# A sparse attention and feed-forward kernel: the first 22 loads wait for the one three ahead

## The chip, the cores and the metric

The kernel runs on one core of a Trainium2 chip. The metric is the device time of one execution in microseconds. The five engines of the core are named as in the profile: PE (TensorE; PEld are its weight loads), DVE (VectorE), ACT (ScalarE), POOL (GpSimd) and SP (SyncE). SP only issues transfers here; 16 DMA engines carry them out.

## The reference

Attention over q, k, v of shape (8 batches, 8 heads, 576 positions, 64), then a two-matrix feed-forward block over all 4608 tokens of width 512.

```python
scores = q @ k.T / sqrt(64)
# heads 0-3: 0 <= i - j < 32         (local)
# heads 4-7: i >= j and i % 32 == j % 32   (strided)
attn = softmax(where(mask, scores, -1e9))
x = (attn @ v) as 4608 x 512
h = x @ w_in                       # 512 x 2048
g = where(h >= 1, h, where(h <= -1, 0, (h + 1)**2 / 4))
out = g @ w_out                    # 2048 x 512
```

## The kernel before

All of it runs in one pass over the batches on one core. The queries and keys of a batch come in four tiles (`load_qk`: two for the local heads, two for the strided ones, 576 and 604 KB), the values in four parts for batch 0 (`load_v`: 768, 384, 384 and 320 KB). The weights come as 16 tiles of 128 rows of the hidden layer, each in two halves of 512 KB: half 0 of tile f belongs to w_in, half 1 to w_out (`load_w(f, i)`). They arrive as 64-bit words and are turned into two rounded parts by a chain of five steps on ACT, DVE and POOL: `conv_a` (L457, ACT) and `conv_l` (L461, ACT), `conv_b` (L465, DVE), `conv_c` (L469, POOL), then `conv_d` (L478) and `conv_e` (L482, DVE). Only then can PE use the tile.

Attention of a batch goes score (L592, PE) - mask, maximum, exponential, sum, norm (DVE, ACT, POOL) - transpose (L719, PE) - copy out (L729) - values (L779, PE) - copies into the feed-forward's input, high part (L841, ACT) and low part (L850, DVE). PE then does the first matrix (`up`, L887) and the second (`down`, L947) for the first 512 tokens while further weights are still being converted, and after that the other tokens, in part from combined weight blocks that were stored to DRAM (L1040, L1135). In the first microseconds PE also multiplies zeros (L577, L607).

The order of all instructions is written out by hand: the body runs under a manual schedule, and the long string AGENDA lists the steps with the time at which each is placed between the matrix multiplications. Each engine works through its own queue in that order. All loads are issued by SP, in one queue, in the order in which the program calls them. The first 22 loads are issued ahead of everything else, in this order: the four qk tiles of batch 0; half 0 of weight 0 (it is held until the second qk tile has landed, by a one-element copy on ACT, L435); two parts of v; half 0 of weight 1; two parts of v; half 0 of weight 2; half 1 of weights 0, 1, 2; both halves of weight 3; two qk tiles of batch 1; both halves of weights 4 and 5. The calls are these:

```python
for p in range(4):
    load_qk(0, p)
load_w(0, 0, loaded[0, 1, "qk"][0:1, 0, 0:1])
load_v(0, 0)
load_v(0, 1)
load_w(1, 0)
...
```

In the agenda the conversions by ACT come as A0.0, A1.0, A2.0, A3.0, A0.1, A3.1, A4.0, A1.1 (tile and half); these are its first L457 instructions, in this order.

Of the kernel before, what the change touches and what calls it, by code (L numbers as in the profile page):

```python
# [19 lines left out]
ST = 32  # L20
WR = 7
GATE, ROUNDED = 0.31, 1.62

AGENDA = """
-66.69 0Zs0:17 0o0 0s0 0o1 0i0 0X0 0s1 0i1 0S0 0o3 0g1 0x1 0s2 0Zv0:3 0Zf0:3 0m2 0e0 0a1 A0.0 0s3 0i3 0e1 0x2 0q0
# [263 lines left out]
def tile_sparse_attention_then_ffn(  # L289
# [14 lines left out]
    nc = tc.nc  # L304
# [81 lines left out]
    for i in range(IL):  # L386
        part = slice(i * QL, (i + 1) * QL)
        for n0, n1, off in ((0, SLOTS, ST),) if i else ((0, 1, 0), (1, SLOTS, ST)):
            t = m_loc[part, n0:n1]
# [4 lines left out]
    for i in range(IS):  # L394
        t = m_str[i * QS:(i + 1) * QS]
# [20 lines left out]
    wt, raws, pieces = {}, {}, {}  # L416
    PLACES = (6, 7, 8, 9, 10, 11, 12, 13, 14, 15, 12, 13, 14, 15)
    SUMS_AT = (("X1a", "X1b", "w0", "w1", "w0", "w1", "w0", "w1"), ("X0b", "X0a", "X0b", "X0a", "w11", "w12", "w13", "w14"))
    w_v = w.bitcast(U32).rearrange("f p (i e t) -> f p i e t", i=2, t=2)
# [4 lines left out]
    def place(u, shape, dtype, name):  # L424

        return slot(f"w{u // 2 + NP * (u % 2)}", shape, dtype, name)

    def weight(f, i, h=slice(None)):
        return wt[i, f // 2][:, h, f % 2] if i else wt[i, f // 2][:, f % 2, h]

    def load_w(f, i, after=None):
        if i == 0:
            raws[f] = place(PLACES[f], [P, 2, DM, 2], U32, f"raw_{f}")
        if after is not None:
            nc.scalar.copy(raws[f][0:1, i, 0:1, 0].bitcast(F32), after)  # L435
        nc.sync.dma_start(raws[f][:, i], w_v[f][:, i])
        pieces[f, i] = [(raws[f][:, i], slice(0, DM))]

    def load_piece(f, i, k=0, pool=qk_p, tag="qk", of=1):
# [79 lines left out]
    def load_qk(b, p):  # L519
        src = qk_l[b, p] if p < 2 else qk_s[b, p - 2]  # L520
        if b == 0 and p >= 2:
            t = place(NF + 1 - p, [P, 2, src.shape[2]], F32, f"qk_{b}_{p}")
        else:
            t = qk_p.tile([P, 2, src.shape[2]], F32, tag="qk", name=f"qk_{b}_{p}")
        nc.sync.dma_start(t, src)
        loaded[b, p, "qk"] = t

    def load_v(b, u, k=None):

        local, b0, nb = UNITS[u]  # L530
        if k is not None:
            b0, nb = b0 + k * VB, min(VB, nb - k * VB)
        src = (v_l if local else v_s)[b][:, b0:b0 + nb]
        if b == 0 and u in (0, 3):
            t = place(5 if u else 4, list(src.shape), F32, f"v_{b}_{u}")
        else:
            t = v_p.tile([P, VB, 2, D], F32, tag="v", name=f"v_{b}_{u}_{k}")[:, :nb]
        nc.sync.dma_start(t, src)
        for n in range(nb):
            loaded[b, local, b0 + n] = t[:, n]  # L540

    def fetch_qk(b, p0):
        for p in (p0, p0 + 1):
            if b < B and (b, p, "qk") not in loaded:
                load_qk(b, p)

    def fetch_v(b, *parts):
        for u, k in parts:
            if 0 < b < B and (b, UNITS[u][0], UNITS[u][1] + k * VB) not in loaded:
                load_v(b, u, k)  # L550
# [612 lines left out]
    with tc.manual_schedule():  # L1163
# [6 lines that stand above are left out]
        load_v(0, 2)  # L1170
        load_v(0, 3)
        load_w(2, 0)
        for f in range(3):
            load_w(f, 1)
        for i in range(2):
            load_w(3, i)
        for p in range(2):
            load_qk(1, p)
# [57 lines left out]
        for f in range(NF):  # L1236
            t = 4 * (f - NF)
# [6 lines left out]
        t, last = 0, None  # L1244
# [82 lines left out]
```

## Time and profile before

| | us |
|---|---|
| median of 3 runs | 802.49 |
| lowest, highest run | 801.35, 804.53 |
| span of the profiled execution | 801.3 |
| PE busy | 791.8 (99%) |
| DVE busy | 621.0 (77%) |
| ACT busy | 504.9 (63%) |
| POOL busy | 259.3 (32%) |

The span runs from the first to the last instruction of the one execution that was profiled; its own time outside the span is not listed apart, and the lowest of the runs, 801.35, is next to it. The rows below come from that execution. In a row of an engine the first number is the start in us from the span's start, the second how long the row lasts; in square brackets stands how long the engine was idle before it, and what released it. SPq is SP's issuing of a transfer, not the transfer; the time of a transfer is the time from issue to landing.

### The profile page before, as it was taken

Reading aid. Unit: us, or ns where it says so; the run is one execution under the profiler, and the core shown is the slowest. Engines: PE = TensorE matmul, PEld = TensorE weight load, DVE = VectorE, ACT = ScalarE, POOL = GpSimd, SP = SyncE. Lnnn points to the kernel's source line nnn. Section 1 sums busy time; section 2 is a strip of 40 time slices with the busy share of each in tenths; the row PEclk is TensorE's granted clock in tenths of the full one; section 3 lists DMA queues with packets and bytes.
Section 4 is the critical chain, followed back from the end, with each engine's and each line's share of the span. In section 5 each row is a group of like instructions: output and inputs, shape, how many; then the busy total and the mean of one; then the engine's idle time right before and its main releaser. Section 6 shows DMA issues by size and latency. Waiting matters only on the chain.

```text
span 801.3 us, 17840 instructions
## 1 busy us (share of the span) xinstructions
PE 791.8 (99%) x6921; PEld 647.5 (81%) x6921; DVE 621.0 (77%) x881; ACT 504.9 (63%) x857; POOL 259.3 (32%) x203
## 2 busy tenths in 40 slices
PE   8999999999999999999999999999999999999998
PEld 6778887778887888888888888888888888888886
DVE  5899879998999999978689786675786854566673
ACT  5899854566764555677665456777544667775442
POOL 5456344897584320022141102132424001224000
PEclk9999999999999999999999999999999999999999
DMA  9948888899898999888889778777777676666665
GB/s 347 406 192 292 302 290 303 277 301 309 288 315 302 298 309 361 267 291 273 261 241 309 230 225 268 249 233 214 221 245 244 212 239 193 194 193 188 216 209 164
DMA packets 107699, 209.78 MB, mean 262 GB/s; under 512 B 17760, under 2 KB 33376, under 8 KB 105568
## 3 DMA queue, kind: packets, MB, share of 16 engines
q1 hardware_dynamic: 100560, 179.15, 70.2%
q10 hardware_dynamic: 7056, 29.49, 9.5%
q8 instruction: 55, 0.90, 0.4%
q14 instruction: 28, 0.23, 0.1%
HBM read 161.94 MB, written 46.66 MB: 260 GB/s over the span
## 4 chain that ended last, share of the span: by engine, by line
PE 96%; DMA 1%; DVE 1%; ACT 1%; issue 0%; SPq 0%; DVEq 0%
PE yo L1135 22%; PE y L1040 16%; PE h L887 16%; PE zo L1135 11%; PE z L1040 8%; PE o L947 6%; PE xo L1135 6%; PE x L1040 4%; PE xp L779 4%; PE sc L592 3%; DMA raw<-in_w 1%; DMA qk<-in_qk_l 1%; PE tp L719 1%; DVE xq_b L850 0%; ACT pT L729 0%
## 5 line engine op out<-in xcount | busy, mean ns | idle before, releaser
L1135 PE MATMUL yo<-hl,wr 128*128 128x512 f32 x768 | 177.6, 390 | 0.0
L1135 PEld LDWEIGHTS yo<-hl,wr 128*128 128x128 f32 x768 | 143.6, 188 | 30.8 <-DVE hl L997 0.9
L1040 PE MATMUL y<-x,wr 128*128 128x512 f32 x576 | 139.9, 389 | 0.0
L1040 PEld LDWEIGHTS y<-x,wr 128*128 128x128 f32 x576 | 108.0, 188 | 22.5
L887 PE MATMUL h<-xq_a,w 128*128 128x512 f32 x384 | 123.2, 394 | 1.1 <-DVE g L897 1.0
L1096 POOL TENSOR_TENSOR ga<-gb,ga 128x1024 f32<-128x1024 f32 x17 | 44.1, 2600 | 235.9 <-DVE ga L897 175.5
L997 DVE TENSOR_TENSOR hl<-ga,hl 128x1024 fp32r<-128x1024 f32 x48 | 63.7, 1341 | 36.9 <-ACT hl L996 36.7
L1135 PE MATMUL zo<-hl,wr 128*128 128x512 f32 x384 | 89.3, 391 | 0.0
L887 PEld LDWEIGHTS h<-xq_a,w 128*128 128x128 f32 x384 | 72.0, 188 | 17.3 <-DVE g L897 1.6
L1135 PEld LDWEIGHTS zo<-hl,wr 128*128 128x128 f32 x384 | 71.7, 188 | 15.6 <-DVE hl L997 0.6
L996 ACT CAST hl<-ga 128x1024 fp32r<-128x1024 f32 x48 | 49.9, 1050 | 51.1 <-PE yo L1135 16.3
L887 PE MATMUL h<-xq_b,w 128*128 128x512 f32 x192 | 73.6, 391 | 0.1
L1040 PE MATMUL z<-x,wr 128*128 128x512 f32 x288 | 73.5, 391 | 0.0
L1040 PEld LDWEIGHTS z<-x,wr 128*128 128x128 f32 x288 | 53.8, 188 | 11.3
L894 ACT ACTIVATE tmp<-tmp 128x512 f32<-128x512 f32 x96 | 60.7, 633 | 3.0
L997 DVE TENSOR_TENSOR hl<-gb,hl 128x1024 fp32r<-128x1024 f32 x36 | 48.7, 1367 | 14.4 <-ACT hl L996 14.3
L996 ACT CAST hl<-gb 128x1024 fp32r<-128x1024 f32 x36 | 37.7, 1056 | 31.3 <-PE zo L1135 15.3
L504 POOL TENSOR_TENSOR st<-st 128x256 f32<-128x256 f32 x48 | 50.6, 1056 | 13.5 <-DVE st L705 5.9
L897 DVE SCALAR_TENSOR_TENSOR ga<-ga,tmp 128x512 f32<-128x512 f32 x48 | 33.0, 688 | 28.2 <-ACT tmp L894 28.0
L891 ACT ACTIVATE u<-h,half 128x512 f32<-128x512 f32 x48 | 33.0, 687 | 31.8 <-PE h L887 23.5
L469 POOL TENSOR_TENSOR raw<-raw 128x512 uint32<-128x512 uint32 (+1 forms) x34 | 35.9, 1068 | 42.5 <-DVE raw L465 16.3
L682 POOL TENSOR_TENSOR pr<-pr,st 128x384 f32<-128x384 f32 (+3 forms) x18 | 26.8, 1490 | 63.7 <-DVE st L678 60.6
(124 smaller groups left out, 1409.2 us busy)
## 6 DMA issues: line engine op xcount, KB each, us to landing
wr<-ks SPq DMA_DIRECT2D x224, 256.0 KB, 4.0
wr<-kq SPq DMA_DIRECT2D x168, 256.0 KB, 3.4
ks<-st ACTq DMA_DIRECT2D x16, 1024.0 KB, 7.0
raw<-in_w SPq DMA_DIRECT2D x30, 512.0 KB, 9.6
qk<-in_qk_s SPq DMA_DIRECT2D x16, 604.0 KB, 6.3
qk<-in_qk_l SPq DMA_DIRECT2D x16, 576.0 KB, 6.2
kq<-w ACTq DMA_DIRECT2D x16, 512.0 KB, 3.8
v<-in_v_l SPq DMA_DIRECT2D x21, 384.0 KB, 5.6
```

The source lines that it names most:

```text
L469: nc.gpsimd.tensor_tensor(out=raw[:, :, 1], in0=raw[:, :, 1], in1=raw[:, :, 0], op=ALU.add)
L504: eng.tensor_tensor(out=st[:, to, 1], in0=st[:, x, 1], in1=st[:, y, 1], op=op)
L887: nc.tensor.matmul(o_ps[c, f], weight(f, 0, h)[:, x, e:e + P], xq[c][y][:, cc], start=first and n == 0, stop=last and n == len(todo) - 1)
L891: nc.scalar.activation(u, h, AF.Relu, bias=half, scale=0.5)
L894: nc.scalar.activation(u, u, AF.Square)
L897: nc.vector.scalar_tensor_tensor(out=to, in0=h, scalar=1.0, in1=u, op0=ALU.max, op1=ALU.min)
L947: nc.tensor.matmul(o_ps["o"][d], weight(f, 1, h)[:, x, e:e + P], gs[y], start=f == 0 and n == 0, stop=f == NF - 1 and n == 2)
L996: nc.scalar.copy(t[:, 0], src)
L997: nc.vector.tensor_tensor(out=t[:, 1], in0=src, in1=t[:, 0].bitcast(F32), op=ALU.subtract)
L1040: nc.tensor.matmul(to, w_[:, a, c * P:(c + 1) * P], xc[m][:, b, c], start=m in (1, 2, 5) and c + q == 0, stop=c == 1 and q == 2, skip_grou ...
L1096: eng.tensor_tensor(out=to, in0=x, in1=y, op=op)
L1135: nc.tensor.matmul(to, w_[jj][:, a, d * P:(d + 1) * P], t[:, b, jj], start=m in (1, 2, 5) and k + jj + q == 0, stop=k == NP // 2 - 1 and j ...
```

## The change

Every load of `load_w`, `load_qk` and `load_v` now goes through a helper, `begin`, which issues it as before and keeps a list of the loads so far. For the loads with index 5 to 21 in that list, it adds a dependency on the load three earlier: the load is issued only when that one has landed. Loads 0 to 4 and those from 22 on get none. `load_piece` is not touched.

```diff
+AHEAD, GATED = 3, (5, 22)
...
+    begun = []
+
+    def begin(to, src):
+
+        ins = nc.sync.dma_start(to, src).ins
+        if GATED[0] <= len(begun) < GATED[1]:
+            tc.add_manual_dep(ins, begun[-AHEAD].name, mybir.DependencyInfo(mybir.DependencyClass.Sync, mybir.DependencyReason.DATA), reason="loads ahead")
+        begun.append(ins)
...
-        nc.sync.dma_start(raws[f][:, i], w_v[f][:, i])
+        begin(raws[f][:, i], w_v[f][:, i])
...
-        nc.sync.dma_start(t, src)
+        begin(t, src)
...
-        nc.sync.dma_start(t, src)
+        begin(t, src)
```

## Rows read from the trace of the kernel before

**Rows 1.** The page: busy time of each engine, and the chain's shares by engine.
```profile
PE 791.8 (99%) x6921; PEld 647.5 (81%) x6921; DVE 621.0 (77%) x881; ACT 504.9 (63%) x857; POOL 259.3 (32%) x203
...
PE 96%; DMA 1%; DVE 1%; ACT 1%; issue 0%; SPq 0%; DVEq 0%
```

**Rows 2.** By windows: length, busy us of PE, PEld, DVE, ACT, POOL, PE clock, DMA share, GB/s.
```profile
0.00:27.78 27.78, 23.01 (x544) 17.24 (x544) 18.23 (x43) 15.91 (x47) 14.13 (x35) 1.00 0.95 365
27.78:780.00 752.22, 751.07 (x6300) 615.93 (x6301) 594.07 (x831) 483.78 (x805) 245.16 (x168) 1.00 0.80 261
780.00:801.30 21.30, 17.69 (x79) 14.31 (x77) 8.67 (x9) 5.17 (x6) 0.00 (x0) 0.97 0.52 168
```

**Rows 3.** The chain that ended last, in order of time: start, us, what.
```profile
6.26 5.37 DMA raw<-in_w
...
27.78 3.24 PE h L887 x13
```

**Rows 4.** Waits of SP's queue, 0 to 40 us: total, times, longest.
```profile
SPq L436 <- DMA raw<-in_w: 9.4, 10, 1.5
```

**Rows 5.** SP's issues: loads 2, 3, 12, 13, 14, 18, 21, 22, 26, a later one.
```profile
1.65 0.42 SPq L525 DMA_DIRECT2D qk<-in_qk_s  x1
2.11 0.43 SPq L525 DMA_DIRECT2D qk<-in_qk_s  x1
...
11.65 0.33 SPq L436 DMA_DIRECT2D raw<-in_w  x1
13.55 0.33 SPq L436 DMA_DIRECT2D raw<-in_w  x1
14.53 0.33 SPq L436 DMA_DIRECT2D raw<-in_w  x1
...
19.36 0.33 SPq L436 DMA_DIRECT2D raw<-in_w  x1
...
23.17 0.33 SPq L436 DMA_DIRECT2D raw<-in_w  x1
24.49 0.33 SPq L538 DMA_DIRECT2D v<-in_v_l  x1
...
30.43 0.33 SPq L436 DMA_DIRECT2D raw<-in_w  x1
...
59.79 0.33 SPq L436 DMA_DIRECT2D raw<-in_w  x1
```

**Rows 6.** Issue to landing, median us: loads 2, 3, those at 59.79, 64.20.
```profile
qk<-in_qk_s SPq DMA_DIRECT2D x1, 604.0 KB, 6.0
qk<-in_qk_s SPq DMA_DIRECT2D x1, 604.0 KB, 7.1
...
raw<-in_w SPq DMA_DIRECT2D x1, 512.0 KB, 4.2
...
raw<-in_w SPq DMA_DIRECT2D x2, 512.0 KB, 5.6
```

**Rows 7.** By windows, columns as in rows 2: around the first bytes of 59.79.
```profile
59.70:60.70 1.00, 1.00 (x65) 0.94 (x66) 1.00 (x4) 1.00 (x3) 0.00 (x0) 1.00 0.00 0
60.70:60.80 0.10, 0.10 (x24) 0.10 (x16) 0.10 (x2) 0.10 (x1) 0.00 (x0) 1.00 2.35 246
```

**Rows 8.** ACT in order of time: conversions of weights 0, 2, 3, 4.
```profile
11.65 0.68 ACT L457 ACTIVATE raw<-raw 128x512 f32<-128x512 f32 x1 [1.50 <-DMA raw<-in_w]
...
20.08 0.69 ACT L457 ACTIVATE raw<-raw 128x512 f32<-128x512 f32 x1
...
27.85 0.68 ACT L457 ACTIVATE raw<-raw 128x512 f32<-128x512 f32 x1
...
31.37 0.70 ACT L457 ACTIVATE raw<-raw 128x512 f32<-128x512 f32 x1
```

**Rows 9.** PE in order of time: first values of batch 0, scores of batch 1.
```profile
15.68 1.50 PE L779 MATMUL xp<-pT,v 64*64 64x32 f32 x63 [0.24 <-ACT pT L729]
...
30.95 1.17 PE L592 MATMUL sc<-qk 64*32 64x64 f32 x96
```

## The prediction

> **What bounds the kernel now.** I read the page's busy times and chain first. TensorE (PE) is busy 791.8 of 801.3 us, and the chain that ended last is 96% PE and 1% DMA [rows 1]; the span leaves 9.5 us in which PE is idle. The view by windows says where these are [rows 2]: 4.8 us before 27.78 (27.78 - 23.01), 1.2 us from there to 780, and 3.6 us in the tail, with a granted clock of 1.00 in the first two and 0.97 in the last. So from 27.78 on PE works off a fixed amount of work, and the end moves only if the changed loads move that starting point or tear a hole behind it. The loads in question all go out in the first 24 us.
>
> In this beginning the chain passes through one load: the first half of weight tile 0, issued at 6.26, lands after 5.37 us, and PE's row that opens its unbroken work starts at 27.78 [rows 3]. ScalarE (ACT) had waited 1.50 us for that load when it began its conversion at 11.65 [rows 8]. The later conversions in those rows show no wait for a DMA, so the loads behind weight 0 come early.
>
> **Numbering.** In SP's order load 0 to 3 are the four qk tiles of batch 0, 4 is weight tile 0 (first half), 5 and 6 are v, 7 weight 1, 8 and 9 v, 10 weight 2, 11 to 13 the second halves of weights 0 to 2, 14 and 15 weight 3, 16 and 17 qk of batch 1, 18 to 21 weights 4 and 5. Loads 0 to 4 get no wait; 5 to 21, that is 17 loads, get one.
>
> **The change part by part.** *The added waits.* Before, the loads aren't unlimited either: SP waited for landings of weight loads ten times in the first 40 us [rows 4], and load n goes out right behind the landing of load n-8: weight 0 (load 4) lands at 6.26 + 5.37 = 11.63, load 12 is issued at 11.65 [rows 3, 5]. So the change takes the number in flight from eight to three, and a wait costs SP 0.02 us between landing and issue. It also lets me read landings from issues: by the issues of loads 13, 14, 18, 22 and 26, loads 5, 6, 10, 14 and 18 land at about 13.53, 14.51, 19.34, 24.47 and 30.41 [rows 5].
>
> *Does the DMA run dry with three in flight?* The DMA engines are 95% busy at 365 GB/s in the first 27.78 us, ramp included [rows 2]. In the steady part loads 11 to 14, four of 512 KB, land between 19.34 and 24.47 [rows 5]: 5.13 / 4 = 1.28 us each. When load n-3 lands, loads n-2 and n-1 are queued: 2.56 us of transfers for 512 KB loads; for load 10, with v loads of 384 and 320 KB ahead, 2.56 x 704/1024 = 1.76 us. Against this stands the time from a release to the first bytes of a new load: a load issued into an idle queue at 59.79 [rows 5] has no DMA activity until 60.70 and is active in 60.70 to 60.80 [rows 7], so 0.9 to 1.0 us, plus 0.02. Both 2.56 and 1.76 exceed it, so the queue still holds work when the new load joins, and the landings stay where they are: 0 us.
>
> *Upper bound.* No row shows how much of a load's fixed cost is hidden behind only two others. Take it that none is: the load at 59.79, with another only some 0.5 us behind, needs 4.2 us to land [rows 6], against 3 x 1.28 = 3.84 us in steady flow. Give each gated load 4.22 us after the landing of the one three ahead. From load 4, load 7 lands at 15.85, 10 at 20.07, 13 at 24.29, 16 at 28.5; from load 5, 8 at 17.75, 11 at 21.97, 14 at 26.19, 17 at 30.4 (30.6 for its 576 KB); from load 6, 9 at 18.73, 12 at 22.95, 15 at 27.2, and 18 at 31.4, or 31.9 if it must also land 1.28 us after 17. The needs: weight 2 (load 10) at 20.08, weight 3 (14) at 27.85, weight 4 (18) at 31.37 [rows 8]; v (5) at 15.68, both qk of batch 1 (16, 17) at 30.95 [rows 9]. Load 5 waits for load 2, landed at 1.65 + 6.0 = 7.65 [rows 5, 6]: 7.67 + 4.2 + 0.64 for its further 256 KB is 12.5, earlier than the 13.53 that its queue gave it. Only load 18 comes late, by 0.5 us. ACT's order behind it (more conversions and the gate) feeds PE, so I count it whole: +0.5 us.
>
> *Lower bound.* A gain could come only through weight 0, for which ACT waited. Load 3 landed at 2.11 + 7.1 = 9.2 [rows 5, 6], so at the steady pace weight 0 could land at 10.5 instead of 11.63, if the loads behind it were what held it back. Passed on whole that is -1.2 us. But load 5, released at 7.67, brings its first bytes at about 8.6, while weight 0 is still under way; it is beside weight 0 in either kernel, and only the loads behind it are away. Between the ends I take 0: the rows of the rate and of the first bytes are nearer to this case than a lone load is.
>
> On this I weighed the Trainium skill, "DMA: Bandwidth & Descriptors", section "Rules for kernel authors": issue a DMA early and wait late, so that its fixed cost is overlapped; this speaks against the change, which issues 17 loads later. The same page ("Anatomy of one DMA") fits some 2.0 us fixed plus bytes over 436 GB/s, for the gpsimd path; an estimate by it is 3.2 us for 512 KB, under the 4.2 us measured here, and three in flight at 1.28 us each would still hide it, so the sum by the page is also 0.
>
> *What is queued behind the waiting SP.* Load 21 can now go out only when load 18 has landed, at about 30.4, where before it went out at 23.17 [rows 5]. Behind it stand two v loads of batch 1, the first of which (load 22) went out at 24.49, and the weights from number 6 on. Load 26, issued at 30.43 before, now goes out after loads 21 to 25, at SP's 0.33 to 0.43 us each [rows 5]: some 2 us later. But it stood behind seven others, about 9 us of transfers, and three of them are still ahead of it in flight or just issued; the queue is shorter and its landing doesn't move. SP has only loads to issue in this stretch, and no compute engine's queue holds an added wait.
>
> *Sum:* 0 us, bounds -1.2 and +0.5, against the profiled span of 801.3. The median of the runs is 802.49, 1.2 us above that span, with runs from 801.35 to 804.53. I predict 802.5. A difference of under 0.5%, 4 us, can't be told from none on this kernel.
>
> **Rivals.** *Weight 0 lands earlier* because fewer loads share the DMA engines. For it: 2.4 us lie between the landings of loads 3 and 4 where 1.28 would do. Against it: loads 4, 5 and 6 land in the order of issue, so a load behind took little from one ahead; and VectorE is busy 18.2 of the first 27.78 us [rows 2], so not all of ACT's earlier start is passed on. At most -1.2 us: 801.3.
>
> By the Trainium skill ("DMA: Bandwidth & Descriptors", "Queues, rings and completion order") each DMA engine takes descriptors in ring order; by that rule this rival returns nothing, and the order of the landings here agrees.
>
> *The slowest DMA engine runs dry at every release* (slower). Its place is ACT's in-order queue, at the conversions of weights 2 and 4. It decides from the round trip r of a load: load 10 lands at 11.63 + 2r, so above 4.2 us the conversion at 20.08 is late; load 18, four round trips behind load 6, costs 4 us when 14.51 + 4r = 31.37 + 4, r = 5.2 us. With 5.6 us, the median of a pair issued at 64.2 beside other traffic [rows 6], load 18 lands at 36.9: +5.5 us, 808.0. Against it: that traffic is absent here, and the first bytes come after 0.9 us. A mild form, some tenths per release, is the bound's +0.5: 803.0.
>
> *The waits do nothing*, because the kernel's own eight-ahead waits stand in for them, or they bind to an issue and not to a landing: 802.5.
>
> **Chances.** Landings that matter don't move: 0.76, 802.5. Weight 0 earlier: 0.08, 801.3 to 802. Mild starvation: 0.10, 803. Full starvation: 0.03, 808. Waits without effect: 0.03. All but full starvation stay within 4 us; it and a small remainder on either side for causes I don't see make slower 0.04 and faster 0.02, the same 0.94. Range: the bounds give 801.3 to 803.0, and the runs shown scatter from 1.1 below to 2.0 above their median; together 800.5 to 804.8.
>
> **What would show it.** SP's issues of loads 5, 6, 7 at about 7.7, 9.2, 11.65 and of load 21 near 30.4; about 4 us from issue to landing; landings of loads 10 and 18 still at 19.3 and 30.4; a DMA rate like that of before between 10 and 30 us; PE unbroken from about 27.8. ACT waiting for a weight at 20.08 or 31.37, or a clearly lower rate, would show starvation; weight 0 landed by 10.6 and PE unbroken from 27 or earlier, the first rival. The prediction is wrong if the start of PE's unbroken work moves by over 4 us or PE shows as much new idle time after 30 us.

## The result and the profile after

The changed kernel takes 811.09 us (median of 5 runs, 810.05 to 811.6) against 803.12 for the kernel before on the same chip (5 runs, 801.35 to 804.53): a ratio of 1.0096, interval 1.0084 to 1.0108. The change makes it 8.0 us slower by the medians, 7.7 us by the ratio. I had forecast no change, 802.5, and no more than 804.8. The profiled span went from 801.3 to 808.6.

The page of the changed kernel, the lines that answer to [rows 1] (engines' busy us; the chain's shares). Its line numbers are ten higher than before: L467 here is L457 there.

```profile
PE 793.0 (98%) x6921; PEld 646.5 (80%) x6921; DVE 621.7 (77%) x881; ACT 505.8 (63%) x857; POOL 259.7 (32%) x203
...
PE 86%; DMA 7%; DVE 4%; POOL 1%; ACT 1%; issue 0%; SPq 0%; ACTq 0%; POOLq 0%; DVEq 0%
```

PE does as many instructions as before; DMA went from 1% to 7% of the chain. The view by windows of the changed kernel, columns as in [rows 2]:

```profile
0.00:27.78 27.78, 22.95 (x545) 16.99 (x545) 18.25 (x43) 16.09 (x47) 14.09 (x35) 1.00 0.85 291
27.78:60.00 32.22, 26.26 (x241) 19.32 (x241) 23.82 (x49) 24.17 (x43) 12.32 (x11) 1.00 0.87 312
...
100.00:400.00 300.00, 298.81 (x3284) 243.25 (x3283) 263.77 (x394) 188.30 (x335) 133.50 (x103) 1.00 0.89 298
...
780.00:808.60 28.60, 24.96 (x111) 20.33 (x109) 14.83 (x16) 9.43 (x11) 0.00 (x0) 0.98 0.53 177
```

The loss has one place. PE's idle time is 4.8 us before 27.78 as in [rows 2], then 6.0 us (32.22 - 26.26) between 27.78 and 60, where it had none; after 60 it is what it was (1.2 us up to 400, 3.6 in the tail). With 1.2 us more of busy time (793.0 against 791.8) that is the 7.3 us of the span. In the first 27.78 us the DMA engines now move 291 GB/s instead of 365.

SP's issues in the changed kernel, loads 5, 6, 7, 9, 15, 18, 21; each row also dates the landing of the load three ahead:

```profile
7.71 0.33 SPq L436 DMA_DIRECT2D v<-in_v_l  x1
9.19 0.36 SPq L436 DMA_DIRECT2D v_None<-in_v_l  x1
11.37 0.33 SPq L436 DMA_DIRECT2D raw<-in_w  x1
...
14.89 0.33 SPq L436 DMA_DIRECT2D v<-in_v_s  x1
...
24.43 0.33 SPq L436 DMA_DIRECT2D raw<-in_w  x1
...
30.88 0.33 SPq L436 DMA_DIRECT2D raw<-in_w  x1
...
36.98 0.33 SPq L436 DMA_DIRECT2D raw<-in_w  x1
```

From load 6 on each third load: 9.19, 14.89, then load 12 at 19.32 (in the chain below), 24.43, 30.88, 36.98. A round trip of three loads takes 5.7, 4.4, 5.1, 6.5 and 6.1 us where 3.84 would have kept the pace. Load 18 lands at 36.96 instead of 30.41. The chain of the changed kernel is made of these round trips (start, us, what):

```profile
9.19 5.64 DMA v_None<-in_v_l
...
14.89 4.40 DMA v<-in_v_s
...
19.32 5.09 DMA raw<-in_w
...
24.43 6.44 DMA raw<-in_w
...
30.88 6.08 DMA raw<-in_w
```

ACT in the changed kernel: the conversions of weights 0, 2 and 4 and, at the end, of weight 7, each with ACT's idle time and the transfer that ended it:

```profile
11.37 0.68 ACT L467 ACTIVATE raw<-raw 128x512 f32<-128x512 f32 x1 [1.06 <-DMA raw<-in_w]
...
21.55 0.67 ACT L467 ACTIVATE raw<-raw 128x512 f32<-128x512 f32 x1 [1.63 <-DMA raw<-in_w]
...
36.98 0.67 ACT L467 ACTIVATE raw<-raw 128x512 f32<-128x512 f32 x1 [3.80 <-DMA raw<-in_w]
...
48.78 0.67 ACT L471 ACTIVATE raw<-raw 128x512 uint32<-128x512 uint32 x1 [2.45 <-DMA raw<-in_w]
```

PE in the changed kernel: its first feed-forward row, the scores of batch 1, the first row of the second matrix, and two later rows of the first matrix:

```profile
24.67 0.73 PE L897 MATMUL h<-xq_a,w 128*128 128x512 f32 x2
...
32.40 0.82 PE L602 MATMUL sc<-qk 64*32 64x64 f32 x48 [1.39 <-DMA qk<-in_qk_l]
34.60 0.72 PE L602 MATMUL sc<-qk 64*32 64x64 f32 x48 [1.38 <-DMA qk<-in_qk_l]
...
39.38 0.50 PE L957 MATMUL o<-gh,w 128*128 128x512 f32 x1 [1.11 <-ACT w L488]
...
50.62 0.50 PE L897 MATMUL h<-xq_a,w 128*128 128x512 f32 x1 [0.60 <-ACT w L488]
...
52.20 0.73 PE L897 MATMUL h<-xq_a,w 128*128 128x512 f32 x2 [0.85 <-DVE w L492]
```

Weight 2 (load 10), needed at 20.08 in [rows 8], holds ACT for 1.63 us, but PE's first feed-forward row comes at 24.67, where the kernel before had it at 24.75: that stall is absorbed. What costs is the qk of batch 1 (1.39 + 1.38 us of PE), then weight 4, for which ACT waits 3.80 us (behind it PE waits 1.11 us at 39.38 for a converted weight, and 0.38 and 0.26 us more by 48), and at 48.78 even a load that has no added wait, a half of weight 7: it went out only after SP was through with the gated ones, at 38.78 instead of 28.58 (behind it PE waits 0.60 and 0.85 us). These waits add up to PE's 6.0 us.

### The profile page after: what moved, and what is told of

The parts are those of the page before. It is cut to its first block, busy times and chain, and to the rows that moved or that the text cites. A ratio compares the mean times of both kernels' runs of the same rounds, so it can differ in the third digit from the quotient of the medians.

```text
span 808.6 us, 17838 instructions
## 1 busy us (share of the span) xinstructions
PE 793.0 (98%) x6921; PEld 646.5 (80%) x6921; DVE 621.7 (77%) x881; ACT 505.8 (63%) x857; POOL 259.7 (32%) x203
## 4 chain that ended last, share of the span: by engine, by line
PE 86%; DMA 7%; DVE 4%; POOL 1%; ACT 1%; issue 0%; SPq 0%; ACTq 0%; POOLq 0%; DVEq 0%
PE yo L1145 21%; PE y L1050 16%; PE h L897 12%; PE zo L1145 11%; PE z L1050 8%; PE xo L1145 5%; PE x L1050 4%; PE o L957 4%; DMA raw<-in_w 3%; PE xp L789 3%; PE sc L602 2%; DMA wr<-kq 2%; DVE st L522 1%; DMA qk<-in_qk_s 1%; DMA v_None<-in_v_l 1%; DMA v<-in_v_s 1%
## 5 line engine op out<-in xcount | busy, mean ns | idle before, releaser
L479 POOL TENSOR_TENSOR raw<-raw 128x512 uint32<-128x512 uint32 (+1 forms) x34 | 36.0, 1068 | 50.6 <-DVE raw L475 15.7
L901 ACT ACTIVATE u<-h,half 128x512 f32<-128x512 f32 x48 | 32.9, 685 | 30.5 <-PE h L897 21.8
L692 POOL TENSOR_TENSOR pr<-pr,st 128x384 f32<-128x384 f32 (+3 forms) x18 | 26.7, 1487 | 63.9 <-DVE st L688 60.8
```

The costliest lines, as they stand in the source:

```text
L479: nc.gpsimd.tensor_tensor(out=raw[:, :, 1], in0=raw[:, :, 1], in1=raw[:, :, 0], op=ALU.add)
L901: nc.scalar.activation(u, h, AF.Relu, bias=half, scale=0.5)
```

## The experiments

Theory A: with three loads in flight the DMA engines run dry in part; a load's fixed cost is not hidden behind two others, so loads land ever later. Theory B: the added dependencies cost by themselves. All kernels differ from the changed one in the line that sets the depth and the first and last gated load, unless a diff shows more. Ratios are to the kernel before, run on the same chip; a difference in us is the ratio's part of 803 us, unless it is said to be one of medians.

**Eight ahead**

```diff
-AHEAD, GATED = 3, (5, 22)
+AHEAD, GATED = 8, (8, 22)
```

> Loads 8 to 21 each get an added dependency on the load eight ahead, nothing else. Theory A (three loads in flight leave DMA engines dry): this names a wait that the kernel before already has (load 12 went out 0.02 us after load 4 landed), so no landing moves: 0.0 us, within 0.3 us of before, loads 10 and 18 landing near 19.3 and 30.4. Theory B (the added dependencies cost by themselves, through SP's queue or semaphores, whatever the depth): 14 of the 17 waits stay, so 14/17 of the 7.3 us between the spans, about +6 us.

Measured: 802.35, ratio 0.9991 (0.998 to 1.0003): no difference. This run can't decide on theory B, though. In both traces SP has 1221 instructions, and those that issue these loads wait for the same landings, so the added dependencies gave no new wait. What the run confirms is that eight in flight is what the kernel before does.

**Four ahead**

```diff
+AHEAD, GATED = 4, (5, 22)
```

> As the change, but four loads in flight instead of three (each load from 5 to 21 waits for the load four ahead). Theory A: in steady flow four loads take 4 x 1.28 = 5.1 us, and the changed kernel's loads took 4.4 to 7.0 us from issue to landing, half of the 512 KB ones over 5.1; so the engines still run dry at times, but lose far less: +1 to +3.5 us. Theory B: as many waits, the same +7 us.

Measured: 803.98, ratio 1.0019 (1.0007 to 1.0031), +1.5 us. One load more in flight gives back four fifths of the loss. Theory B falls here: 17 loads wait, as in the changed kernel, and the price is a fifth. With five ahead, below, 17 such waits cost nothing measurable.

**Only the early loads, only the late loads**

```diff
+AHEAD, GATED = 3, (5, 11)
```

> Only loads 5 to 10 wait for the load three ahead; 11 to 21 don't. Theory A: load 10 (weight 2) lands about 2.2 us late as in the changed kernel (21.5 instead of 19.3) and ACT waits some 1.6 us for it, but PE's first matrix multiplication of the feed-forward starts at 24.7 in both kernels, so that stall is absorbed; the loads behind flow at 1.28 us again but stay up to 2 us late, load 17 (needed at 30.95) at 30.8 or so, load 18 at 32.5 instead of 30.4: +0.5 to +2 us. A rival C, that ACT's wait for weight 2 alone costs the end: +1.6 us or more with PE's first h row moved by as much.

```diff
+AHEAD, GATED = 3, (11, 22)
```

> Only loads 11 to 21 wait for the load three ahead; 5 to 10 don't. Theory A: loads 4 to 10 land as before, weight 2 at 19.3; behind it the lateness grows by what it grew in the changed kernel after load 10: load 17 was 6.0 us late there, load 10 2.2, so 3.8 us at load 17 (lands at 32.4, needed at 30.95) and 4.4 at load 18 (34.8, needed at 31.37); PE stalls for qk of batch 1 and weights 3 and 4: +3.5 to +6 us. Rival C: about 0 to +2 us, since the early part is untouched.

Measured: early only 805.62, ratio 1.004 (1.0021 to 1.006), +3.2 us, above the range I gave; late only 809.0, ratio 1.0065 (1.0038 to 1.0092), +5.2 us. The two add up to 8.4, about the whole, but in part by chance: in the profiled execution of the late run PE also ran at a granted clock of 0.68 and 0.50 of full speed from 32 to 36 us, while the changed kernel kept 1.00. With the early loads alone, ACT's waits and PE's first feed-forward row (start of it):

```profile
21.50 0.65 ACT L467 ACTIVATE raw<-raw 128x512 f32<-128x512 f32 x1 [1.62 <-DMA raw<-in_w]
...
33.39 1.22 ACT L467 ACTIVATE raw<-raw 128x512 f32<-128x512 f32 x2 [1.79 <-DMA raw<-in_w]
```

```profile
24.62 0.72 PE L897 MATMUL h<-xq_a,w 128*128 128x512 f32 x2
...
32.13 0.73 PE L602 MATMUL sc<-qk 64*32 64x64 f32 x48 [0.51 <-DMA qk<-in_qk_l]
```

So rival C falls: PE's first row doesn't move, ACT's wait for weight 2 is absorbed. What costs is that a delay once made is kept: the loads behind flow at full rate again, but later, and weight 4 comes 1.79 us late at ACT, although it isn't gated itself. With the late loads alone it is 4.27 us:

```profile
34.57 1.23 ACT L467 ACTIVATE raw<-raw 128x512 f32<-128x512 f32 x2 [4.27 <-DMA raw<-in_w]
```

**One and two in flight**

```diff
+AHEAD, GATED = 1, (5, 22)
```

> Each load from 5 to 21 waits for the load before it: one load in flight, so the rows show what a lone load costs from issue to landing. By the bound of the prediction 4.2 us for 512 KB, so 4.2 to 4.5 us between landings instead of 1.28; load 18 (needed at 31.37) lands near 70 us and the run is some 40 to 55 us longer. If the 5 to 6.5 us of the changed kernel are what a lone load needs even with nothing beside it, load 18 lands near 85 to 95 us: +55 to +70 us.

```diff
+AHEAD, GATED = 2, (5, 22)
```

> Two loads in flight. Theory A: the queue is dry more often than with three; issue to landing 4.2 to 5 us for two loads, 2.1 to 2.5 us per load against 1.28, 14 loads from 4 to 18: load 18 lands at 41 to 46 instead of 30.4; with the slack of about 1 us, +10 to +16 us. If the loss were a fixed price per wait, it would be the same +7 us as with three.

Measured: one in flight 844.0 in a single run, +41 us between medians; two in flight 818.19 in two runs, ratio 1.0196 (1.0173 to 1.0219), +15.7 us. Neither is a fixed price per wait. A lone load of 512 KB takes 3.6 us from issue to landing, less than the 4.2 that I had read as a lone load's, so load 18 landed at 60.8 and not near 70. The +41 came within the range even so, perhaps because PE's clock adds to it: from 27.78 to 60 us, where PE is idle for 18.3 of 32.2 us, it was granted 0.61 of full speed in the mean (0.82 with two in flight).

**Five in flight** (run last)

```diff
+AHEAD, GATED = 5, (5, 22)
```

> As the change, but five loads in flight. With one, two, three and four in flight the time went up by 41, 15, 8 and 1.0 to 1.5 us. Theory A: five take 6.4 us in steady flow, more than all but two of the loads of the changed kernel needed from issue to landing, so the queue hardly runs dry: 0 to +0.8 us, load 18 landing by 31.5. Theory B (a price per wait) fell with the eight-ahead run and would still say +7 us.

Measured: 802.99, ratio 1.0008 (0.9995 to 1.002): no measurable difference.

The DMA views of these kernels over the stretch in which the gated weight loads were issued, one fence each, for one, two, three (the changed kernel), four, five and eight in flight (the kernel before): the queue's packets, MB and share of 16 engines; then the weight loads and their median us from issue to landing.

```profile
q1 hardware_dynamic: 2304, 8.32, 44.6%
...
raw<-in_w SPq DMA_DIRECT2D x11, 512.0 KB, 3.6
```

```profile
q1 hardware_dynamic: 2220, 7.94, 74.9%
...
raw<-in_w SPq DMA_DIRECT2D x11, 512.0 KB, 4.4
```

```profile
q1 hardware_dynamic: 2128, 7.58, 87.1%
...
raw<-in_w SPq DMA_DIRECT2D x11, 512.0 KB, 5.3
```

```profile
q1 hardware_dynamic: 2037, 7.12, 95.4%
...
raw<-in_w SPq DMA_DIRECT2D x11, 512.0 KB, 6.6
```

```profile
q1 hardware_dynamic: 1823, 6.40, 98.4%
...
raw<-in_w SPq DMA_DIRECT2D x10, 512.0 KB, 7.0
```

```profile
q1 hardware_dynamic: 1432, 4.84, 101.2%
...
raw<-in_w SPq DMA_DIRECT2D x8, 512.0 KB, 10.6
```

| in flight | issue to landing, us | n x 1.28, us | DMA share | load 18 lands, us | time against before, us |
|---|---|---|---|---|---|
| 1 | 3.6 | 1.28 | 44.6% | 60.8 | +41 (one run) |
| 2 | 4.4 | 2.56 | 74.9% | 42.6 | +15.7 |
| 3 | 5.3 | 3.84 | 87.1% | 37.0 | +7.7 (+8.0 by medians) |
| 4 | 6.6 | 5.12 | 95.4% | 33.0 | +1.5 |
| 5 | 7.0 | 6.40 | 98.4% | 31.3 | none measurable |
| 8 | 10.6 | 10.24 | 101.2% | 30.4 | (before) |

This is how to read it: a load may be in flight for as long as n loads need at full pace, n x 1.28; what it takes beyond that is pace lost. The excess is 2.3, 1.8, 1.5, 1.5, 0.6 and 0.4 us. It doesn't vanish where the lone load's 3.6 us fit into n x 1.28, at three, as I had assumed; at five it is still 0.6 us. Five cost no time because this kernel has 1 us to spare: load 18 lands at 31.3, and ACT needs it at 31.37 [rows 8]. The pace itself is not quite kept: with five the queue moved 6.40 MB in the 17.2 us from 11.3 to 28.5, 0.37 MB per us, and in the kernel before 4.84 MB in the 11.9 us from 11.6 to 23.5, 0.41.

**Larger loads**

The next runs ask whether the bytes in flight count or the number of loads. First the two halves of weights 3, 4 and 5 as one load each, without any added wait, then the same with loads from 11 on gated:

```diff
+    def load_both(f):
+        raws[f] = place(PLACES[f], [P, 2, DM, 2], U32, f"raw_{f}")
+        begin(raws[f], w_v[f])
+        for i in range(2):
+            pieces[f, i] = [(raws[f][:, i], slice(0, DM))]
...
-        for i in range(2):
-            load_w(3, i)
+        load_both(3)
...
-            for i in range(2):
-                load_w(f, i)
+            load_both(f)
```

> No added wait; the two halves of weights 3, 4 and 5 come in one load of 1 MB each instead of two of 512 KB. A control for the next run. Half 0 of weight 4 lands with its other half, 1.28 us later than before, at 31.7 where it is needed at 31.37: 0 to +0.7 us against before.

```diff
+AHEAD, GATED = 3, (11, 19)
```

> As the control with 1 MB loads for weights 3, 4, 5, and loads from 11 on wait for the load three ahead, as in the run with late gating (+4 to +6 us). If what counts is how many bytes are queued (theory A), the three in flight are now 2.0 to 2.6 MB in most places, as with four to five of 512 KB, and four cost +1.5 us: +0.7 to +2.5 us against the control. If the number of loads in flight counts, whatever their size (rival D), the same +4 to +6 us against the control.

Measured: control 803.75, ratio 1.001 (0.9997 to 1.0023); gated 807.86, ratio 1.0067 (1.0051 to 1.0083), +4.6 us against the control. By its number this speaks for rival D. But 4.2 of the 4.7 us by which weight 4 came late, against the control, had arisen by load 13, at the halves of weights 0 to 2, which are ahead of the first 1 MB load in the queue. So the pair was repeated with only the stretch of the large loads gated, halves against whole:

```diff
+AHEAD, GATED = 3, (14, 22)
```

> Only loads 14 to 21 (weight 3, qk of batch 1, weights 4 and 5, weights as halves of 512 KB) wait for the load three ahead. In the changed kernel the lateness against before grew from 2.8 us at load 13 to 6.6 at load 18 and 9.8 at load 21, so here load 18 should land some 3 to 4 us late (33.5 to 34.4, needed at 31.37): +2 to +4 us. This is the partner of the next run; both theories expect the same of it.

```diff
+AHEAD, GATED = 3, (14, 19)
```

(with `load_both`)

> Same stretch gated three ahead, but with weights 3, 4 and 5 as loads of 1 MB (its control without waits cost +0.7 us, within noise). The run with these loads gated from load 11 on was late by 4.2 us already at load 13, before the first 1 MB load, and its lateness then stayed at 3.7 to 4.2 up to load 16; so it didn't tell the theories apart. Theory A (bytes queued count): load 17, weight 4, lands at most 1 to 1.5 us later than the 31.0 of the control, +0.3 to +1.8 us. Rival D (the number of loads counts, whatever their size): as the run with halves, +2 to +4 us.

Measured: halves 807.46, ratio 1.0062 (1.0032 to 1.0091), +5.0 us; whole 805.44, ratio 1.0034 (1.0022 to 1.0045), +2.7 us against before and +1.9 against its control. The queue's row from 21 to 28.9 us, with halves, whole, and for the control of the latter; in this stretch both are gated (the last gated load goes out at 28.56 with whole weights, at 32.92 with halves):

```profile
q1 hardware_dynamic: 527, 2.00, 77.7%
```

```profile
q1 hardware_dynamic: 490, 2.48, 89.5%
```

```profile
q1 hardware_dynamic: 590, 3.26, 100.5%
```

With three loads in flight in either, the larger ones move 2.48 MB where the halves move 2.00. Weight 4 lands 1.5 us later than in the control (32.5 against 31.0), which is what theory A said; with halves it is 2.5 us (32.9 against 30.4). The time doesn't decide: the halves cost more than either theory said, and +1.9 us (some 0.5 to 3.3 by the two intervals, from two chips) lies between the two. In part it is another thing: PE's clock in that kernel fell, as the rows in the last section show. So rate and landing speak for the bytes in flight, but it is not shown: with whole weights five loads are gated instead of eight, and a price per gated load (5.0 / 8 = 0.6 us, 1.9 / 5 = 0.4 us) would look much the same.

## Why the prediction was wrong

**The step that failed** is the first term of the sum: "Both 2.56 and 1.76 exceed it, so the queue still holds work when the new load joins, and the landings stay where they are: 0 us." It compared the transfer time queued at a release with the time to a new load's first bytes, and so took a queue that still holds work for a queue at full pace. The premise held more often than not: for nine of the fourteen loads 8 to 21 no part of the load just ahead was through when the first bytes of the new one could come, 0.95 us after its issue as the run with one in flight has it. And yet the queue is busy for only 87.1% and each load takes 5.3 us instead of 3.84. Two things make the loss. From 24 to 36 us the queue of the kernel before and that of the changed kernel moved this (packets, MB, share):

```profile
q1 hardware_dynamic: 1369, 4.85, 101.3%
```

```profile
q1 hardware_dynamic: 871, 3.30, 86.1%
```

Some engines were idle while loads were in flight (86.1 against 101.3%); and while busy they moved less: 3.30 / (0.861 x 12) = 0.32 MB per us against 4.85 / (1.013 x 12) = 0.40. The single packets in the traces say more on the second. Among those of 4 KB and more in these 12 us the middle one takes 0.16 us in both kernels, but in the changed one 115 of 773 take over 0.2 us, up to 1.7, and hold a third of the busy time; before, it is 2 of 962. So the packets aren't slower throughout: one in seven is very long. With one load in flight, in ten loads of 512 KB, 127 of the 197 long packets are in the first quarter of their load, so a load that finds the queue empty starts slowly. That long packets are starts in the changed kernel too is argued, as the traces don't say which engine carried a packet; why a start is slow stays open.

A load's landing is counted in 16 steps, as many as there are DMA engines, and SP waits for the last. In the changed kernel the first and the last step of loads 7 to 21 lie 0.9 to 4.2 us apart (1.5 to 2.5 before), so each release waits for the slowest part of a load. That the engines done early are the idle ones is argued too.

**The upper bound wasn't one.** "Take it that none is" hidden was priced with one load's 4.2 us. A lone load really takes 3.6, so that figure was even too high for a lone load; but two loads beside it add to the time instead of hiding it: 5.3 us, with single ones up to 7.0. The rows to take it from stood in the trace: the pair at 64.20 with a median of 5.6 [rows 6] was a case of few loads in flight, and I set it aside because of other traffic. There was none to speak of: from 65 to 68 us the only DMA queue that moved anything was that of the loads, and it was as far from full pace as in the changed kernel (packets, MB, share):

```profile
q1 hardware_dynamic: 188, 0.71, 85.2%
```

Its figure was right to 0.3 us, though that near only by luck: two in flight throughout gave 4.4.

**The rival** "runs dry at every release" came nearest, at a chance of 0.03; that it happens at every release is more than the runs show. Its turning point, a round trip of 5.2 us for 4 us of loss, and its price of +5.5 us at 5.6 us describe the result well: load 18 was forecast there for 36.9 and landed at 36.96. The price came out higher: of the 7.3 us by which the span grew, PE's waits make 6.0, and 1.45 of these come behind load 18, with weight 7; why PE is busy for 1.2 us more no run shows. "Its landing doesn't move", said of load 26 behind the waiting SP, was wrong: it landed at 50.0 instead of 40.0, because the queue ahead of it had fallen behind.

**What held.** That PE is the bound and the loss comes from holes behind 27.78; that it goes through ACT's order and the qk of batch 1; that the kernel before already kept eight in flight; that the wait itself is free, as five ahead shows. PE's unbroken work starts earlier than I read, at 24.75 with the first feed-forward row: 27.78 is only where the chain enters PE. The absorbed stall at weight 2 I had not seen: the early part had more slack than the row at 20.08 says.

**Weight 0 earlier** was nearly worthless: it was issued at 6.42 and landed by 11.37, in 4.9 us instead of 5.37, and with nothing at all behind it, one in flight, ACT still began its conversion at 11.37. Fewer loads behind it gave 0.3 us of the 1.2 in the bound.

The Trainium skill's rule that spoke against the change ("DMA: Bandwidth & Descriptors", "Rules for kernel authors": issue early, wait late) was borne out here: loads issued later landed later, +8.0 us. The same page's fit ("Anatomy of one DMA", for the gpsimd path) of 2.0 us plus bytes over 436 GB/s gives an estimate of 3.2 us for a lone 512 KB, and the run with one in flight shows 3.6 on SP's queue. What went wrong was mine, in the sum by the page as in the other: neither figure says how many loads hide it.

## What to carry to other kernels

The number of transfers needed in flight is not the lone transfer's time divided by the time per transfer (3.6 / 1.28, three): here it took five loads of 512 KB, 2.5 MB, for no loss of time, with 1 us to spare, and four lost 1.5 us. Price a shorter queue from rows where few transfers were in flight, all of them, and not from the time to first bytes. And a delay isn't caught up as long as the stream of loads stays full (in the changed kernel to some 57 us): look for the tightest consumer anywhere behind it, not at the gated loads alone.

## What the hardware showed beside this

In the kernel with whole weights gated from load 14, PE's granted clock (1.00 is full speed) fell after a pause (columns as in [rows 2]):

```profile
34.00:36.00 2.00, 0.73 (x2) 0.30 (x2) 2.00 (x5) 2.00 (x4) 1.51 (x2) 1.00 1.00 388
36.00:38.00 2.00, 1.95 (x6) 1.61 (x7) 1.97 (x3) 1.97 (x5) 1.89 (x2) 0.70 0.99 355
38.00:40.00 2.00, 2.00 (x7) 1.06 (x6) 1.97 (x5) 1.97 (x4) 0.54 (x2) 0.50 1.02 416
40.00:44.00 4.00, 4.00 (x63) 3.38 (x63) 3.85 (x10) 3.77 (x8) 2.08 (x2) 0.97 1.03 418
```

PE is busy for 0.73 of 2 us, then works at 0.70 and 0.50, its 1.2 GHz level, and a pair of matrix multiplications of one shape takes 1.05 us where it took 0.63 before the pause:

```profile
32.68 0.63 PE L903 MATMUL h<-xq_a,w 128*128 128x512 f32 x2
...
36.87 1.05 PE L963 MATMUL o<-gh,w 128*128 128x512 f32 x2
```

The changed kernel, with more idle time in all but in other places, kept 1.00 from 0 to 60 us. So a hole torn into PE's work can cost more than its length. It need not: with five in flight the clock fell to 0.64 and 0.51 from 24 to 28 us, and the run was no longer for it by any amount that could be measured. And a lone load's time by size, in the run with one in flight (v loads; median us from issue to landing), 2.8 us for 320 KB and 4.4 for 768 KB, grows by 1.6 us for 448 KB, slower than the 1.28 us per 512 KB of the full stream. That is one load of each size, and lone loads of 512 KB took 3.5 to 4.3 us:

```profile
v<-in_v_s SPq DMA_DIRECT2D x1, 320.0 KB, 2.8
...
v<-in_v_l SPq DMA_DIRECT2D x1, 768.0 KB, 4.4
```
